# Attention forward in a transformer block: a fixed software pipeline with three score slots, value products two units behind, and the output turned by DMA

## The chip, the cores and the metric

The kernel runs on one core of a Trainium2 chip. The metric is the device time of one execution in microseconds (us). Before the change the median was 5007.97 us (three runs, 4999.35 to 5011.92).

Engines in the text: PE multiplies matrices, ACT evaluates exponentials, DVE and POOL do elementwise work, SP issues DMAs. PEld stands for PE's loading of weights. SBUF is the working memory; PSUM holds matmul results. A bank here is a piece of PSUM of 512 f32 columns, and the tile pools of both kernels come to eight of them.

## The reference

One block of a conditioned transformer, forward and backward: layer norm, attention with 32 heads of 16 channels over 2048 tokens, a squared-ReLU feed-forward, and the gradients of all of it. The change touches the attention forward alone:

```python
qkv = (x @ wqkv).reshape(B, S, 3, H, Dh)                    # S = 2048, H = 32, Dh = 16
scores = jnp.einsum('bhqd,bhkd->bhqk', q, k) * Dh ** (-0.5)
p = softmax(scores, axis=-1)
o = jnp.einsum('bhqk,bhkd->bhqd', p, v)
```

## The kernel before

Heads are handled four at a time (8 groups `hg`), queries in four blocks `qc` of 512, keys in sixteen tiles `kt` of 128. One such triple is a *unit*; there are 512. The *lag* is the number of units by which the value products run behind the scores. Per unit PE makes four score tiles (keys x queries). A head fills 32 of PE's 128 rows, so each score is a row-tiled matmul. ACT takes two score tiles per exponential (128x1024, two PSUM banks). PE then adds four value products, each 32 output columns wide (column-tiled), into one accumulator bank. `vaug` carries a column of ones, so the sum for the softmax comes along as a 17th row of each head.

```python
psS = tile_pool(name="psS", bufs=2, space=PSUM)     # two score slots of two banks
psO = tile_pool(name="psO", bufs=2, space=PSUM)     # two accumulators
psT = tile_pool(name="psT", bufs=1, space=PSUM)     # for the turn
for hg in range(HG):
    # ... load qt_sb, kt_sb of the group
    for qc in range(QC):
        oacc = psO.tile([P, 512], F32, tag="oacc")
        for kt in range(TT):
            ET = ework.tile([P, 4, 512], BF, tag="ET")
            for pair in range(2):
                ps = psS.tile([P, 2, 512], F32, tag="psST")
                for hi in range(2):
                    hq = 2 * pair + hi
                    PE.matmul(ps[:, hi, :], kt_sb[32*hq:32*hq+32, ...], qt_sb[32*hq:32*hq+32, ...],
                              tile_position=(32 * hq, 0))                         # L299
                ACT.activation(ET[:, 2*pair:2*pair+2, :], ps[:], AF.Exp, scale=SCALE)   # L302
            for hq in range(4):
                PE.matmul(oacc[32*hq:32*hq+32, :], lhsT, ET[:, hq, :],
                          start=(kt == 0), stop=(kt == TT - 1), tile_position=(0, 32 * hq))  # L306
        ostage = ...; DVE.tensor_copy(ostage[:], oacc[:])
        # ... rows of sums by DMA to rrows
        for qi in range(4):                              # turn the block: queries back to partitions
            pt = psT.tile([P, P], F32, tag="posT")
            PE.transpose(pt[:], ostage[:, qi*P:(qi+1)*P], identf[:])              # L317
            DVE.tensor_copy(O_un[...], pt...)                                     # L320
# ... for each token tile: transpose the sums, reciprocal, O_tok = O_un * r_inv
```

The order of instructions on each engine is not the program's order. A scheduler sets it: with two slots it issues the scores of one pair, then the value products of the pair before, and so on.

## Time and profile before

| stage | from to, us | length | bound by |
|---|---|---|---|
| preparation, projections | 0 to 292 | 292 | |
| attention forward | 292 to 1570 | 1278 | a loop between PE and ACT |
| feed-forward, its backward | 1570 to 2572 | 1002 | |
| attention backward | 2572 to 4720 | 2148 | |
| rest | 4720 to 5010 | 290 | |

The table of stretches of the kernel before. Columns: from:to, length, busy us (and instructions) of five engines, PEclk = granted PE clock as a share of full speed, DMA share, GB/s.

```profile
core 0: us, PE busy (x) PEld busy (x) DVE busy (x) ACT busy (x) POOL busy (x), PEclk, DMA share, GB/s
...
292.00:1570.00 1278.00, 1224.18 (x4236) 287.06 (x4237) 62.18 (x180) 1047.77 (x1025) 0.00 (x0) 0.50 0.02 6
...
2572.00:4720.00 2148.00, 1945.42 (x10240) 368.51 (x10239) 1222.26 (x1024) 1100.73 (x1185) 152.85 (x110) 0.61 0.73 136
```

In the forward ACT is busy 1048 of 1278 us and the matmul records cover 1224. The granted clock is 0.50 throughout. The page's groups, where the numbers after the bar are busy us and mean ns of one, then idle us before them and who ended it:

```profile
L302 ACT ACTIVATE ET<-psST 128x1024 bf16<-128x1024 f32 x1024 | 1046.5, 1024 | 228.4 <-PE psST L299 226.3
...
L299 PE MATMUL psST<-qt_sb,kt_sb 32*128 32x512 bf16 x2048 | 658.3, 603 | 17.3 <-DMA kt_sb<-KtP 17.3
L306 PE MATMUL oacc<-ET,vaug 128*32 128x512 bf16 x2048 | 626.1, 604 | 45.9 <-ACT ET L302 4.5
```

ACT idles 228 us, nearly all of it for scores. The timeline shows how (start, length, engine, line, what, count):

```profile
start us, us, engine line op out<-in xcount [idle before <-releaser]
800.10 1.02 ACT L302 ACTIVATE ET<-psST 128x1024 bf16<-128x1024 f32 x1
800.14 0.61 PE L306 MATMUL oacc<-ET,vaug 128*32 128x512 bf16 x2
...
800.69 0.61 PE L299 MATMUL psST<-qt_sb,kt_sb 32*128 32x512 bf16 x2
...
801.23 0.61 PE L306 MATMUL oacc<-ET,vaug 128*32 128x512 bf16 x2
801.39 2.04 ACT L302 ACTIVATE ET<-psST 128x1024 bf16<-128x1024 f32 x2 [0.28 <-PE psST L299]
...
801.77 0.61 PE L299 MATMUL psST<-qt_sb,kt_sb 32*128 32x512 bf16 x2
...
802.47 0.61 PE L306 MATMUL oacc<-ET,vaug 128*32 128x512 bf16 x2
...
803.72 1.02 ACT L302 ACTIVATE ET<-psST 128x1024 bf16<-128x1024 f32 x1 [0.28 <-PE psST L299]
```

The value products at 800.14 start just after an exponential that began at 799.07 ends (its record lasts 1.02). The scores at 800.69 follow. The exponential of those scores begins at 801.39, after an idle 0.28, and two of them run. The whole repeats after 2.33 us: 801.39 to 803.72. The chain is exponential ends, value pair, score pair, exponential: 0.06 + 0.55 + 0.70 + 1.02 = 2.33. PE alternates between the two tile forms four times a unit, at 0.54 us each.

The waits view (who waited for whom, us in total, times, longest):

```profile
ACT ET L302 <- PE psST L299: 226.3, 536, 1.8
...
PE psST L299 <- DMA kt_sb<-KtP: 17.3, 1, 17.3
```

The second line is the start of the stage: the first keys arrive late, behind two weight loads of 1.8 MB each.

### The profile page before, as it was taken

What the parts mean: (1) busy time and instruction counts of PE and PEld (TensorE: products, weight loads), DVE (VectorE), ACT (ScalarE), POOL (GpSimd) and SP (SyncE); (2) the same over time, 40 slices, a digit from 0 to 9 for tenths busy, and PEclk for the clock granted to TensorE, in tenths of its full rate; (3) what the DMA queues carried; (4) which work ended last, traced back from release to release, by engine and by line L of the source; (5) the groups of instructions that cost most, each with busy time, mean ns of one, the idle gap of its engine ahead of it and who ended that gap; (6) DMA issues with size and microseconds to landing.
All of it is one profiled execution on the core that took longest, in us unless ns stands there. A gap on an engine that the chain in (4) does not pass through costs nothing.

```text
span 5010.0 us, 48266 instructions
## 1 busy us (share of the span) xinstructions
PE 4158.7 (83%) x18556; PEld 1052.9 (21%) x18629; DVE 2069.8 (41%) x3264; ACT 2232.8 (45%) x2462; POOL 274.0 (5%) x282
## 2 busy tenths in 40 slices
PE   4789999999997872866579999998989999989766
PEld 1222222222222321322221111111111111111122
DVE  7610000000004752720336555555555555555473
ACT  0058888888884000000025555545554554555411
POOL 2000000000000000001310000010000000000000
PEclk7865555555555886966855565666565655666687
DMA  3220000000001243365467867777686877677513
GB/s 110 82 79 9 9 1 9 9 9 8 2 1 42 110 129 90 89 204 173 133 148 132 159 127 150 128 134 143 125 153 123 153 124 147 127 134 130 123 56 92
DMA packets 1212437, 489.34 MB, mean 98 GB/s; under 512 B 1144611, under 2 KB 1174823, under 8 KB 1210669
## 3 DMA queue, kind: packets, MB, share of 16 engines
q1 hardware_dynamic: 1189550, 455.84, 41.5%
q0 software_dynamic: 6144, 28.32, 1.9%
q10 hardware_dynamic: 16512, 2.10, 0.3%
q8 instruction: 146, 2.39, 0.2%
q14 instruction: 85, 0.70, 0.0%
HBM read 124.35 MB, written 80.37 MB: 41 GB/s over the span
## 4 chain that ended last, share of the span: by engine, by line
PE 33%; ACT 8%; DVE 5%; DMA 3%; issue 3%; SPq 1%; POOL 0%; ACTq 0%; DVEq 0%; POOLq 0%
PE psS_u L708 8%; PE accVK L736 8%; ACT E_u L710 7%; PE psD_u L714 6%; PE dqacc L762 5%; PE accVK L739 4%; DVE dS_u L716 3%; DMA dsT<-dS_u 1%; SPq L919 1%; DMA stld<-stok_st 0%; DVE dh1acc L831 0%; DVE dqkv_tok L823 0%; DMA out_dram<-w2blk 0%; ACT vktmp L747 0%; POOL dOs_tokpad L595 0%
## 5 line engine op out<-in xcount | busy, mean ns | idle before, releaser
L716 DVE TENSOR_TENSOR dS_u<-psD_u,E_u 128x1024 bf16<-128x1024 f32 x1024 | 1222.3, 1222 | 965.6 <-ACT E_u L710 780.2
L710 ACT ACTIVATE E_u<-psS_u 128x1024 bf16<-128x1024 f32 x1024 | 1018.6, 1023 | 886.3 <-PE psS_u L708 881.4
L302 ACT ACTIVATE ET<-psST 128x1024 bf16<-128x1024 f32 x1024 | 1046.5, 1024 | 228.4 <-PE psST L299 226.3
L714 PE MATMUL psD_u<-iv,ido 32*128 32x512 bf16 x2048 | 643.3, 540 | 107.7 <-ACT E_u L710 91.9
L299 PE MATMUL psST<-qt_sb,kt_sb 32*128 32x512 bf16 x2048 | 658.3, 603 | 17.3 <-DMA kt_sb<-KtP 17.3
L306 PE MATMUL oacc<-ET,vaug 128*32 128x512 bf16 x2048 | 626.1, 604 | 45.9 <-ACT ET L302 4.5
L708 PE MATMUL psS_u<-ik,iq 32*128 32x512 bf16 x2048 | 601.6, 532 | 22.5 <-ACT E_u L710 14.8
L309 DVE COPY ostage<-oacc 128x512 f32<-128x512 f32 x32 | 22.1, 692 | 1083.7 <-PE oacc L306 1083.7
L739 PE MATMUL accVK<-E_u,dOs_tok 128*16 128x512 bf16 x2048 | 462.9, 554 | 0.0
L762 PE MATMUL dqacc<-dsT,KS_tok 128*32 128x512 bf16 x2048 | 427.9, 605 | 12.5 <-DMA dsT<-dS_u 9.8
L736 PE MATMUL accVK<-dS_u,qz_14655 128*32 128x512 bf16 x1024 | 316.8, 543 | 35.5 <-DVE dS_u L716 35.3
L736 PE MATMUL accVK<-dS_u,qz_14654 128*32 128x512 bf16 x1024 | 303.7, 557 | 26.8 <-DVE dS_u L716 26.7
L708 PEld LDWEIGHTS <-iq 32*128 32x128 bf16 x2048 | 126.1, 96 | 663.8 <-issue 650.3
L306 PEld LDWEIGHTS <-vaug 128*32 128x32 bf16 x2048 | 151.7, 102 | 466.1 <-issue 437.5
L570 ACT ACTIVATE w1blk<-aw_0_13090 128x512 bf16<-128x512 f32 x1 | 0.6, 597 | 556.2 <-PE aw_0_13090 L566 556.2
L748 POOL TENSOR_TENSOR dVKacc<-dVKacc,vktmp 128x512 f32<-128x512 f32 x96 | 121.3, 1264 | 1910.0 <-ACT vktmp L747 1910.0
L714 PEld LDWEIGHTS <-ido 32*128 32x128 bf16 x2048 | 144.2, 100 | 331.6 <-issue 309.3
L299 PEld LDWEIGHTS <-kt_sb 32*128 32x128 bf16 x2048 | 111.4, 99 | 478.0 <-issue 478.0
L490 PE MATMUL pds<-gfT,w2T 128*128 128x512 bf16 x219 | 54.4, 400 | 109.6 <-DVE dzT L493 79.5
L736 PEld LDWEIGHTS <-qz_14655 128*32 128x32 bf16 x1024 | 59.1, 99 | 312.4 <-issue 311.9
L736 PEld LDWEIGHTS <-qz_14654 128*32 128x32 bf16 x1024 | 56.1, 99 | 295.8 <-issue 295.8
L262 PE MATMUL ppad<-xn1T,wpadT 128*128 128x512 bf16 x376 | 99.1, 409 | 21.7 <-DVE stagep L265 16.2
(1253 smaller groups left out, 2931.6 us busy)
## 6 DMA issues: line engine op xcount, KB each, us to landing
dzld<-dztok_st POOLq DMA_DIRECT2D x32, 448.0 KB, 3.7
dzld<-dztok_st SPq DMA_DIRECT2D x32, 448.0 KB, 3.6
dsT<-dS_u SPq DMA_TRANSPOSE x512, 4.3
rT_st<-rT SPq DMA_DIRECT2D x4, 1792.0 KB
rtok_st<-rtok SPq DMA_DIRECT2D x16, 448.0 KB, 2.5
stok_st<-stok SPq DMA_DIRECT2D x16, 448.0 KB
rTb<-rT_st SPq DMA_DIRECT2D x4, 1792.0 KB
rtokb<-rtok_st SPq DMA_DIRECT2D x16, 448.0 KB, 4.0
```

Of the source, the lines that this page charges most:

```text
L262: PE.matmul(pp[:], wpadT[:, ic, which, hg, :], h1T[:, ic, qc * 512:(qc + 1) * 512], start=(ic == 0), stop=(ic == DC - 1))
L299: PE.matmul(ps[:, hi, :], kt_sb[32 * hq:32 * hq + 32, kt * P:(kt + 1) * P], qt_sb[32 * hq:32 * hq + 32, qc * 512:(qc + 1) * 512], start=Tr ...
L302: ACT.activation(ET[:, 2 * pair:2 * pair + 2, :], ps[:], AF.Exp, scale=SCALE)
L306: PE.matmul(oacc[32 * hq:32 * hq + 32, :], lhsT, ET[:, hq, :], start=(kt == 0), stop=(kt == TT - 1), tile_position=(0, 32 * hq), skip_grou ...
L708: PE.matmul(psS[:, hi, :], st["q"][r:r + 32, qt * P:(qt + 1) * P], st["k"][r:r + 32, kc * 512:kc * 512 + 512], start=True, stop=True, tile ...
L710: ACT.activation(E_u[:, 2 * pair:2 * pair + 2, :], psS[:], AF.Exp, scale=SCALE)
L714: PE.matmul(psD[:, hi, :], st["do"][r:r + 32, qt * P:(qt + 1) * P], st["v"][r:r + 32, kc * 512:kc * 512 + 512], start=True, stop=True, til ...
L716: DVE.tensor_tensor(dS_u[:, 2 * pair:2 * pair + 2, :], psD[:], E_u[:, 2 * pair:2 * pair + 2, :], ALU.mult)
L736: PE.matmul(acc[32 * hq:32 * hq + 32, :], st["qz"][:, qt, hq, :], dS_u[:, hq, :], start=(qi == 0), stop=False, tile_position=(0, 32 * hq), ...
L739: PE.matmul(acc[32 * hq:32 * hq + DH, :], dOs_tok[:, qt, (hg * 4 + hq) * DH:(hg * 4 + hq + 1) * DH], E_u[:, hq, :], start=False, stop=(qi ...
L748: POOL.tensor_tensor(dst, dst, tmp[:], ALU.add)
L762: PE.matmul(acc[32 * hq:32 * hq + 32, :], KS_tok[:, kc * 4 + kt, h * DH:h * DH + 32], tT[:, hq * 4 + kt, :], start=(kc == 0 and kt == 0), ...
```

## The change

Its intent: cut the loop, so that ACT never waits. Three score slots take six banks. The two accumulators take the other two of the eight, so no bank is left for the turn (the transposition of a finished block, queries back to partitions). It goes to DMA, with a bf16 cast on POOL before it. The order on PE and ACT is fixed: both score pairs of unit u, then all four value products of unit u-2.

```diff
-        ework = ... tile_pool(name="phCe", bufs=3)
+        ework = ... tile_pool(name="phCe", bufs=4)
-        psS = ... tile_pool(name="psS", bufs=2, space=PSUM)
+        psS = ... tile_pool(name="psS", bufs=3, space=PSUM)
-        psT = ... tile_pool(name="psT", bufs=1, space=PSUM)
-        O_un = big.tile([P, TT, D], BF, name="O_un")
+        O_un = big.tile([P, TT, HG, P], BF, name="O_un")
+        def fscore(u):   # two pairs: row-tiled scores, exponential each (as before)
+        def fpv(u):      # four column-tiled value products (as before); at the block's end:
                 DVE.tensor_copy(ostage[:], oacc[:])
+                POOL.tensor_copy(obf[:], ostage[:])
-                for qi in range(4):
-                    PE.transpose(pt[:], ostage[:, qi * P:(qi + 1) * P], identf[:])
-                    DVE.tensor_copy(dst, src)
+                SP.dma_start(out=O_un[:, qc * 4:(qc + 1) * 4, hg, :], in_=obf[:], transpose=True)
+        with tc.manual_schedule(engines={PE.engine, ACT.engine}):
+            for u in range(NF + 2):
+                if u < NF:
+                    ...  # load the next head group in time
+                    fscore(u)
+                if u >= 2:
+                    fpv(u - 2)
```

Cut: the loads, and the final scaling, which reads the wider `O_un` and puts its transposes into the accumulators' banks.

More of the change, by code (lines that the diff above doesn't have):

```diff
@@ L277, with fload @@
         wk = ph.enter_context(tc.tile_pool(name="phC", bufs=2))
-        ework = ph.enter_context(tc.tile_pool(name="phCe", bufs=3))
+        ework = ph.enter_context(tc.tile_pool(name="phCe", bufs=4))
         big = ph.enter_context(tc.tile_pool(name="phCbig", bufs=1))
-        psS = ph.enter_context(tc.tile_pool(name="psS", bufs=2, space=bass.MemoryType.PSUM))
+        psS = ph.enter_context(tc.tile_pool(name="psS", bufs=3, space=bass.MemoryType.PSUM))
         psO = ph.enter_context(tc.tile_pool(name="psO", bufs=2, space=bass.MemoryType.PSUM))
-        psT = ph.enter_context(tc.tile_pool(name="psT", bufs=1, space=bass.MemoryType.PSUM))
         rrows = big.tile([P, n], F32, name="rrows")
-        O_un = big.tile([P, TT, D], BF, name="O_un")
-        for hg in range(HG):
+        O_un = big.tile([P, TT, HG, P], BF, name="O_un")
+        funits = [(hg, qc, kt) for hg in range(HG) for qc in range(QC) for kt in range(TT)]
+        fh, fe, fcur = {}, {}, {}
+        def fload(hg):
             qt_sb = wk.tile([P, n], BF, name="qt_sb", tag="qt_sb")
@@ L290 @@
             SP.dma_start(out=kt_sb[:], in_=KtP[hg])
-            for qc in range(QC):
-                oacc = psO.tile([P, 512], F32, name="oacc", tag="oacc")
-                for kt in range(TT):
-                    ET = ework.tile([P, 4, 512], BF, name="ET", tag="ET")
-                    for pair in range(2):
-                        ps = psS.tile([P, 2, 512], F32, name="psST", tag="psST")
-                        for hi in range(2):
-                            hq = 2 * pair + hi
-                            PE.matmul(ps[:, hi, :], kt_sb[32 * hq:32 * hq + 32, kt * P:(kt + 1) * P],
-                                      qt_sb[32 * hq:32 * hq + 32, qc * 512:(qc + 1) * 512],
-                                      start=True, stop=True, tile_position=(32 * hq, 0))
-                        ACT.activation(ET[:, 2 * pair:2 * pair + 2, :], ps[:], AF.Exp, scale=SCALE)
-                    for hq in range(4):
-                        h = hg * 4 + hq
-                        lhsT = vaug[:, kt].rearrange("p h c -> p (h c)")[:, h * (DH + 1):h * (DH + 1) + 32]
-                        PE.matmul(oacc[32 * hq:32 * hq + 32, :], lhsT, ET[:, hq, :],
-                                  start=(kt == 0), stop=(kt == TT - 1), tile_position=(0, 32 * hq), skip_group_check=True)
@@ new lines, in fload @@
+            fh[hg] = (qt_sb, kt_sb)
+        def fscore(u):
+            hg, qc, kt = funits[u]
+            qt_sb, kt_sb = fh[hg]
+            ET = ework.tile([P, 4, 512], BF, name="ET", tag="ET")
+            fe[u] = ET
+            pss = []
+            for pair in range(2):
+                ps = psS.tile([P, 2, 512], F32, name="psST", tag="psST")
+                for hi in range(2):
+                    r = 32 * (2 * pair + hi)
+                    PE.matmul(ps[:, hi, :], kt_sb[r:r + 32, kt * P:(kt + 1) * P],
+                              qt_sb[r:r + 32, qc * 512:(qc + 1) * 512],
+                              start=True, stop=True, tile_position=(r, 0))
+                ACT.activation(ET[:, 2 * pair:2 * pair + 2, :], ps[:], AF.Exp, scale=SCALE)
@@ new lines, in fpv @@
+        def fpv(u):
+            hg, qc, kt = funits[u]
+            if kt == 0:
+                fcur["o"] = psO.tile([P, 512], F32, name="oacc", tag="oacc")
+            oacc = fcur["o"]
+            ET = fe.pop(u)
+            for hq in range(4):
+                h = hg * 4 + hq
+                lhsT = vaug[:, kt].rearrange("p h c -> p (h c)")[:, h * (DH + 1):h * (DH + 1) + 32]
+                PE.matmul(oacc[32 * hq:32 * hq + 32, :], lhsT, ET[:, hq, :],
+                          start=(kt == 0), stop=(kt == TT - 1), tile_position=(0, 32 * hq), skip_group_check=True)
+            if kt == TT - 1:
@@ L308 @@
                 ostage = wk.tile([P, 512], F32, name="ostage", tag="ostage")
                 DVE.tensor_copy(ostage[:], oacc[:])
+                obf = wk.tile([P, 512], BF, name="obf", tag="obf")
+                POOL.tensor_copy(obf[:], ostage[:])
                 for hq in range(4):
@@ L313 @@
                                  in_=ostage[32 * hq + 16:32 * hq + 17, :])
-                for qi in range(4):
-                    t = qc * 4 + qi
-                    pt = psT.tile([P, P], F32, name="posT", tag="posT")
-                    PE.transpose(pt[:], ostage[:, qi * P:(qi + 1) * P], identf[:])
-                    src = pt.rearrange("q (h c) -> q h c", h=4)[:, :, 0:DH]
-                    dst = O_un[:, t, hg * 64:(hg + 1) * 64].rearrange("q (h d) -> q h d", h=4)
-                    DVE.tensor_copy(dst, src)
-        for t in range(TT):
-            pr = psT.tile([P, H], F32, name="prinv", tag="prinv")
-            PE.transpose(pr[:], rrows[0:H, t * P:(t + 1) * P], identf[0:H, 0:H])
-            DVE.reciprocal(r_inv[:, t, :], pr[:])
-            DVE.tensor_tensor(O_tok[:, t, :].rearrange("p (h d) -> p h d", d=DH),
-                              O_un[:, t, :].rearrange("p (h d) -> p h d", d=DH),
-                              r_inv[:, t, :].unsqueeze(2).to_broadcast([P, H, DH]), ALU.mult)
+                SP.dma_start(out=O_un[:, qc * 4:(qc + 1) * 4, hg, :], in_=obf[:], transpose=True)
+        NF = len(funits)
+        fload(0)
+        with tc.manual_schedule(engines={PE.engine, ACT.engine}):
+            for u in range(NF + 2):
+                if u < NF:
+                    if funits[u][1:] == (2, 0) and funits[u][0] + 1 < HG:
+                        fload(funits[u][0] + 1)
+                    fscore(u)
+                if u >= 2:
+                    fpv(u - 2)
+        for t in range(TT):
+            pr = psO.tile([P, 512], F32, name="prinv", tag="oacc")
+            PE.transpose(pr[:, 0:H], rrows[0:H, t * P:(t + 1) * P], identf[0:H, 0:H])
+            DVE.reciprocal(r_inv[:, t, :], pr[:, 0:H])
+            DVE.tensor_tensor(O_tok[:, t, :].rearrange("p (g h d) -> p g h d", g=HG, h=4),
+                              O_un[:, t].rearrange("p g (h c) -> p g h c", h=4)[:, :, :, 0:DH],
+                              r_inv[:, t, :].rearrange("p (g h) -> p g h", g=HG).unsqueeze(3).to_broadcast([P, HG, 4, DH]),
+                              ALU.mult)
         SP.dma_start(out=o_st[:], in_=O_tok[:])
```

## The prediction

It was written before the changed kernel ran.

> What bounds the kernel now. The table of stretches puts the attention forward at 292 to 1570 us, 1278 of 5010 us. There ACT is busy 1048 us, matmuls 1224 us at a granted clock of 0.50. Neither engine is at its limit: the timeline repeats every 2.33 us per unit (four heads, one key tile; 512 units). In it ACT runs two exponentials of 1.02 us and idles 0.28 us for the scores (the waits give 226 us in all), and value products start as an exponential ends. With two score slots this is a loop: exponential ends, value pair (0.55 us), score pair, exponential 0.70 us after that score begins and lasting 1.02: 0.06+0.55+0.70+1.02 = 2.33. PE changes between row-tiled scores and column-tiled value products four times a unit, 0.54 us each: 2.16 us.
>
> What the change does.
> 1. Six banks hold three score slots; a unit's two score pairs stand together, then four value products of two units earlier, whose exponentials are long done. The loop is cut. PE per unit, from groups in the backward, which already has this form: score pair after score pair 0.43, a pair or quad with change of form 0.54: 0.43+0.54+0.54, about 1.5 us, up to 1.7 with weight-load stalls of 0.16.
> 2. ACT then bounds. Its exponential lasts 1.024 us, but in the backward's pairs the second starts 0.904 us after the first (two take 1.94). The Trainium skill, "Perfetto Trace Analysis", section "Optimizing Scalar/DVE Operations", says that half of the profiled access latency overlaps with the next instruction; the trace agrees (1.024 against 0.904). The forward's 1.02 spacing is the score's arrival (0.64 us after its start), not ACT's limit. So a unit should take 1.81 to 1.84 us: 1024 exponentials in about 932 us, against 1275 now. Gain about 340 us.
> 3. A score can start when the exponential three back ends and is needed 0.64 us before its own; three slots leave about 1 us of slack, more than the value quad takes. ACT should not starve.
> 4. PE loses 128 f32 transposes (0.47 us each), DVE 128 copies (0.22); mostly hidden now. Added: 32 casts on POOL (estimate below 1 us, from 0.65 for a bf16 copy) and 32 DMA transposes (4.3 us to landing in the backward), hidden but for the last. The tail from the last value product to O_tok, now 9 us, becomes about 11.
> 5. SBUF placement moves the two feed-forward weight loads (1.8 MB each) from before the first score load to after the stage. Now PE waits 17.3 us for kt_sb behind them; I expect 5 us back. Afterwards they run under the output projection.
> The rest keeps its instructions (ACT and POOL identical, PE and DVE reordered only in the projection): 5008 less 340, less 5, plus some 3.
>
> Predicted: 4666 us, 80% range 4640 to 4765. Faster by over 2%: 0.97; within 2%: 0.025; slower: 0.005.
>
> What would show it. Forward stage about 935 us; ACT busy about 99% of it, exponentials starting every 0.904 to 0.92 us; ACT idle for scores under 10 us; PE matmul busy share down to 75 to 90%, PE waiting for ACT; value products in quads of one modelled length, not two; clock still near 0.5. Backward (2570 to 4740) unchanged in length within 5 us.
>
> What would make it wrong. If every second exponential, which carries an extra wait for ACT's own earlier write, does not overlap with its predecessor, a unit takes 1.93 and the total is about 4730. If no overlap is sustained, 1.02 each: about 4780. If value quads do not run side by side, PE takes 1.95 a unit. The twelve early reciprocal transposes in the last query block could stall PE; late weight loads could delay the layer norm by up to 10 us.

## The result, and the profile after

| | before | after |
|---|---|---|
| median, us | 5009.94 (4 runs) | 4657.15 (4 runs, 4652.79 to 4670.40) |
| ratio | 1 | 0.930 (95% interval 0.9273 to 0.9328) |
| first score to last value product | 1277.6 | 941.4 |
| first to last exponential's start | 1273.9 | 937.1 |
| unit, median | 2.327 | 1.833 |

A ratio is formed from the fast runs of both kernels in the same rounds, so it isn't quite the ratio of the medians quoted. Lengths of stages are taken from the start and end times in the trace.

The stretches after, with the columns of before (forward; attention backward):

```profile
281.40:1223.00 941.60, 869.47 (x4111) 163.68 (x4112) 33.27 (x56) 940.05 (x1025) 19.06 (x31) 0.50 0.05 13
...
2230.00:4370.00 2140.00, 1941.20 (x10162) 366.19 (x10161) 1211.13 (x1015) 1089.05 (x1173) 152.72 (x110) 0.60 0.73 135
```

The profiled execution became 353 us shorter: 336 us in the forward stage and 11 us from its earlier start (281.5 instead of 292.1). The other 7 us lie in stages with unchanged work. From the last value product to the first exponential of the backward it was 988 us in place of 1006, and the exponentials of the backward spanned 2149 in place of 2135. Over all profiled kernels these two lengths scatter from 988 to 1006 and from 2132 to 2158, so nothing is read from that part.

The groups of the page:

```profile
L309 ACT ACTIVATE ET<-psST 128x1024 bf16<-128x1024 f32 x1024 | 938.8, 1770 | 0.0
...
L306 PE MATMUL psST<-qt_sb,kt_sb 32*128 32x512 bf16 x2048 | 622.5, 597 | 79.9 <-DMA kt_sb<-KtP 8.9
...
L320 PE MATMUL oacc<-ET,vaug 128*32 128x512 bf16 x2048 | 316.8, 609 | 0.6 <-ACT ET L309 0.6
```

Two traps stand here. The mean length of an exponential's record is now 1770 ns, though all but nine of the exponentials start 904 to 921 ns after the one before (median 911): the records overlap here, and the spacing, or busy time over count (938.8/1024 = 0.917 us), is what counts. The ends of the records are steadier than their starts: 916 to 918 ns apart. And the score matmuls' records still cover 622 us. The timeline:

```profile
799.64 5.49 ACT L309 ACTIVATE ET<-psST 128x1024 bf16<-128x1024 f32 x5
800.21 0.62 PE L320 MATMUL oacc<-ET,vaug 128*32 128x512 bf16 x4
...
800.77 1.35 PE L306 MATMUL psST<-qt_sb,kt_sb 32*128 32x512 bf16 x4
...
802.05 0.62 PE L320 MATMUL oacc<-ET,vaug 128*32 128x512 bf16 x4
...
802.60 1.35 PE L306 MATMUL psST<-qt_sb,kt_sb 32*128 32x512 bf16 x4
```

ACT runs without a gap. PE gives a value quad, then two score pairs whose records fill 1.35 us because the second pair waits for its slot: in the trace it starts 0.05 us after the end of the exponential three back. The waits in the stage show hardly any of that, and no wait of ACT for scores:

```profile
PE psST L306 <- ACT ET L309: 2.6, 3, 2.0
```

The start, one line of the timeline: PE waits 8.90 us for the first keys instead of 17.31.

```profile
281.46 1.04 PE L306 MATMUL psST<-qt_sb,kt_sb 32*128 32x512 bf16 x6 [8.90 <-DMA kt_sb<-KtP]
```

### The profile page after: what moved, and what is told of

Its sections match the earlier page's. It is cut to its first block, busy times and chain, and to the rows that moved or that the text cites. A ratio compares the mean times of both kernels' runs of the same rounds, so it can differ in the third digit from the quotient of the medians.

```text
span 4656.5 us, 48021 instructions
## 1 busy us (share of the span) xinstructions
PE 3802.4 (82%) x18427; PEld 924.4 (20%) x18501; DVE 2039.2 (44%) x3136; ACT 2125.7 (46%) x2462; POOL 293.9 (6%) x314
## 4 chain that ended last, share of the span: by engine, by line
PE 36%; ACT 8%; DVE 5%; DMA 4%; issue 3%; SPq 1%; POOL 0%; ACTq 0%; DVEq 0%; POOLq 0%
PE psS_u L731 9%; PE accVK L759 9%; ACT E_u L733 7%; PE psD_u L737 6%; PE dqacc L785 6%; PE accVK L762 4%; DVE dS_u L739 3%; DMA dsT<-dS_u 1%; SPq L942 1%; DVE dqkv_tok L846 1%; DMA stld<-stok_st 1%; DVE dh1acc L854 0%; DMA out_dram<-w2blk 0%; ACT vktmp L770 0%; POOL dOs_tokpad L618 0%
## 5 line engine op out<-in xcount | busy, mean ns | idle before, releaser
L309 ACT ACTIVATE ET<-psST 128x1024 bf16<-128x1024 f32 x1024 | 938.8, 1770 | 0.0
L306 PE MATMUL psST<-qt_sb,kt_sb 32*128 32x512 bf16 x2048 | 622.5, 597 | 79.9 <-DMA kt_sb<-KtP 8.9
L320 PE MATMUL oacc<-ET,vaug 128*32 128x512 bf16 x2048 | 316.8, 609 | 0.6 <-ACT ET L309 0.6
L785 PEld LDWEIGHTS <-KS_tok 128*32 128x32 bf16 x2048 | 79.2, 113 | 176.4 <-issue 165.9
```

The costliest lines, as they stand in the source:

```text
L306: PE.matmul(ps[:, hi, :], kt_sb[r:r + 32, kt * P:(kt + 1) * P], qt_sb[r:r + 32, qc * 512:(qc + 1) * 512], start=True, stop=True, tile_posi ...
L309: ACT.activation(ET[:, 2 * pair:2 * pair + 2, :], ps[:], AF.Exp, scale=SCALE)
L320: PE.matmul(oacc[32 * hq:32 * hq + 32, :], lhsT, ET[:, hq, :], start=(kt == 0), stop=(kt == TT - 1), tile_position=(0, 32 * hq), skip_grou ...
L785: PE.matmul(acc[32 * hq:32 * hq + 32, :], KS_tok[:, kc * 4 + kt, h * DH:h * DH + 32], tT[:, hq * 4 + kt, :], start=(kc == 0 and kt == 0), ...
```

## The experiments

The experiments ran in four groups, each on one chip with the kernel before beside it: two slots, both lags and the pairs; the DMA turn alone, with the third slot, the PE turn and the 384 columns; the order left to the scheduler, the changed kernel again and the triples; the 128 columns. Ratios are to that kernel. The runs that the table leaves out stand in their sections below.

| kernel | median, us | ratio | forward stage in the trace, us | unit, us |
|---|---|---|---|---|
| before | 5010 | 1 | 1277.6 | 2.327 |
| changed | 4657 | 0.930 | 941.4 | 1.833 |
| two slots | 4692 | 0.936 | 973.6 | 1.893 |
| lag of one unit | 4668 | 0.931 | 942.0 | 1.833 |
| no lag | 5384 | 1.075 | 1662.0 | 3.240 |
| value products in pairs | 4836 | 0.965 | 1108.2 | 2.160 |
| before + DMA turn | 4916 | 0.981 | 1194.6 | 2.327 |
| before + DMA turn + third slot | 4824 | 0.963 | 1108.4 | 2.160 |
| changed, order left to the scheduler | 4826 | 0.962 | 1108.5 | 2.160 |
| changed, PE turn | 4746 | 0.947 | 1009.3 | 1.808 |

The theory: the loop is cut by having value products far enough behind, PE's four changes of form are halved by grouping, and then ACT's exponentials bound the stage. Rivals: the third slot feeds ACT (A); slots and DMA turn make the gain and the order doesn't (B); grouping is indifferent (C).

### Two score slots

```diff
-psS = tile_pool(name="psS", bufs=3)
+psS = tile_pool(name="psS", bufs=2)
```

> The changed kernel with two score slots in PSUM instead of three, all else as it is. My theory: the lag and the grouping matter, the third slot hardly. Stepping the groups by hand with the measured durations (score 0.64 us before its exponential can start, slot free 1.07 us after its exponential starts, 0.43 us from score pair to score pair, 0.54 us at a change of form), a unit takes 1.85 us instead of 1.81: about 20 us more, 4660 to 4720, with ACT idle 10 to 60 us for scores. Rival A, that the third slot is what keeps ACT fed: most of the gain goes, 4850 or more.

Measured 4691.79 us, ratio 0.936 (0.9338 to 0.9381); the stage is 32 us longer. Rival A falls: with lag and grouping in place the third slot is worth about a tenth of the stage's gain. PE now shows the wait for its slot; the second score pair often starts late:

```profile
701.38 0.62 PE L320 MATMUL oacc<-ET,vaug 128*32 128x512 bf16 x4
...
702.08 0.61 PE L306 MATMUL psST<-qt_sb,kt_sb 32*128 32x512 bf16 x2
702.99 0.61 PE L306 MATMUL psST<-qt_sb,kt_sb 32*128 32x512 bf16 x2 [0.30 <-ACT ET L309]
```

The expectation of ACT's idle time was missed: ACT shows 2 us, not 10 to 60. The loss sits in the spacing (968.8 us busy in place of 938.8), as an exponential whose score is late doesn't overlap with the one before.

### A lag of one unit, and none

```diff
-            for u in range(NF + 2):  ...  if u >= 2: fpv(u - 2)
+            for u in range(NF + 1):  ...  if u >= 1: fpv(u - 1)     # and with 0
```

> The changed kernel with the value products one unit behind the scores instead of two. My theory: the value quad's exponentials end about 0.95 us after its last score starts, PE waits there for half a microsecond that it has to spare, and with three slots ACT still finds a score ready: no change, within 8 us of the changed kernel (4650 to 4668). Rival, that two units of lag are needed: 20 us or more slower.

Measured 4668.38 us, ratio 0.9313 (0.9292 to 0.9334), against 0.930 for the changed kernel; the median is 0.4 us outside of what was expected (4650 to 4668). The stage decides: 942.0 against 941.4 us. One unit of lag is enough, and the second one isn't used.

> The changed kernel with the value products right after their own unit's scores (no lag); three slots, fixed order and DMA turn stay. My theory: the lag is what cuts the loop. PE then waits for both exponentials of the unit and ACT then waits for the next scores: 0.64 + 0.91 + 1.07 + 0.54 = 3.15 us a unit, about 690 us more, 5330 (5250 to 5400), slower than the kernel before. Rival B, that slots and DMA turn make the gain: stays under 4800.

Measured 5384.49 us, ratio 1.0748: slower than the kernel before, with three slots, DMA turn and grouping all in place. Rival B falls. The loop stands in the timeline: PE waits 1.17 us for the exponential before its value products, ACT 1.30 us for the scores after them.

```profile
699.38 1.94 ACT L309 ACTIVATE ET<-psST 128x1024 bf16<-128x1024 f32 x2 [1.30 <-PE psST L306]
...
700.45 0.61 PE L320 MATMUL oacc<-ET,vaug 128*32 128x512 bf16 x2 [1.17 <-ACT ET L309]
...
701.37 0.61 PE L320 MATMUL oacc<-ET,vaug 128*32 128x512 bf16 x2 [0.30 <-ACT ET L309]
...
701.91 0.61 PE L306 MATMUL psST<-qt_sb,kt_sb 32*128 32x512 bf16 x4
...
702.62 1.94 ACT L309 ACTIVATE ET<-psST 128x1024 bf16<-128x1024 f32 x2 [1.30 <-PE psST L306]
```

### Value products in pairs

```diff
-                fscore(u)                 # two pairs
-                fpv(u - 2)                # four products
+                fscore(u, 0); fpv(u - 2, 0)   # a pair each
+                fscore(u, 1); fpv(u - 2, 1)
```

> The changed kernel with the same lag and slots, but the value products in two pairs, one after each score pair, so that PE changes form four times a unit as in the kernel before. My theory: each group costs PE 0.54 us, 2.16 us a unit, and PE bounds instead of ACT: 512 x (2.16 - 1.83), about 170 us more, 4825 (4790 to 4850); ACT idle about 170 us for scores. Rival C, that grouping is indifferent once the loop is cut: 4650 to 4670.

Measured 4836.12 us, ratio 0.965 (0.9631 to 0.9669). The unit is 2.160 us, as four changes of 0.54. Each line below starts 0.54 us after the one above:

```profile
699.83 0.60 PE L306 MATMUL psST<-qt_sb,kt_sb 32*128 32x512 bf16 x2
...
700.37 0.61 PE L320 MATMUL oacc<-ET,vaug 128*32 128x512 bf16 x2
...
700.91 0.61 PE L306 MATMUL psST<-qt_sb,kt_sb 32*128 32x512 bf16 x2
...
701.45 0.61 PE L320 MATMUL oacc<-ET,vaug 128*32 128x512 bf16 x2
...
701.99 0.61 PE L306 MATMUL psST<-qt_sb,kt_sb 32*128 32x512 bf16 x2
```

Rival C falls: a pair and a quad cost PE the same 0.54 us, so half of the groups is half of the time. The Trainium skill, "TensorEngine Tiling (Array Packing)", section "Key Properties", says "Mode switching requires drain"; the trace agrees: at this clock, groups of two and of four, each with a change of form, follow each other by 0.54 us, while quads of one form (`dqacc` in the backward of the kernel before, same clock) follow each other by 0.39 to 0.43 us. ACT's idle time again came out smaller than expected (61 us, not 170), for the reason above.

### The kernel before with the DMA turn alone

```diff
-                for qi in range(4):  PE.transpose(...); DVE.tensor_copy(...)
+                POOL.tensor_copy(obf[:], ostage[:])
+                SP.dma_start(out=O_un[...], in_=obf[:], transpose=True)
```

> The kernel before with only the output's turn moved from PE to DMA; two slots, the scheduler's order of pairs, no fixed order. The prediction called the 128 PE transposes mostly hidden. In the trace of before, the exponentials around each query block's end are spaced up to 2.86 us instead of 1.3: 102 such gaps sum to 76 us beyond the rhythm. If they come from the transposes in PE's order, this kernel gains about 76 us, and some 8 from the weight loads that move away from the start: about 4925 (4905 to 4950). If the transposes were hidden: 5000 or more.

Measured 4915.99 us, ratio 0.9809 (0.979 to 0.9828): clearly below 1, though about the 2% that a verdict asks for. The stage is 83 us shorter while the unit keeps its 2.327 us: all of it comes from the ends of query blocks. ACT's idle time fell by as much, from 228.4 us:

```profile
L302 ACT ACTIVATE ET<-psST 128x1024 bf16<-128x1024 f32 x1024 | 1046.5, 1024 | 145.5 <-PE psST L299 143.3
```

The stage also starts 10 us earlier, since the weight loads moved here too. In the kernel before, such an end reads:

```profile
810.70 2.04 ACT L302 ACTIVATE ET<-psST 128x1024 bf16<-128x1024 f32 x2 [0.28 <-PE psST L299]
...
811.93 0.47 PE L317 MATMUL posT<-identf,ostage 128*128 128x128 f32 x1 [0.25 <-DVE ostage L309]
...
813.41 0.47 PE L317 MATMUL posT<-identf,ostage 128*128 128x128 f32 x1
...
814.52 1.02 ACT L302 ACTIVATE ET<-psST 128x1024 bf16<-128x1024 f32 x1 [1.77 <-PE psST L299]
...
815.43 0.47 PE L317 MATMUL posT<-identf,ostage 128*128 128x128 f32 x1
...
816.37 0.47 PE L317 MATMUL posT<-identf,ostage 128*128 128x128 f32 x1
816.47 1.02 ACT L302 ACTIVATE ET<-psST 128x1024 bf16<-128x1024 f32 x1 [0.93 <-PE psST L299]
...
818.02 2.04 ACT L302 ACTIVATE ET<-psST 128x1024 bf16<-128x1024 f32 x2 [0.53 <-PE psST L299]
```

The exponentials start at 810.70 (two, the second about 1.02 later), 814.52, 816.47 and 818.02: up to 2.8 us apart instead of at most 1.31, while f32 transposes stand between scores on PE. So the transposes were not hidden, as the prediction had said.

### The DMA turn and the third slot, order left to the scheduler; and the changed kernel without its fixed order

```diff
 before + DMA turn, and: psS bufs=2 -> 3, no psT, prinv in psO, ework bufs=3 -> 4
 changed kernel:  with tc.manual_schedule(...):  ->  if True:
```

> The kernel before with the DMA turn and a third score slot, order left to the scheduler, which then runs value pairs three score pairs behind instead of two, but still as alternating pairs. My theory: the loop is cut by the third slot here, and PE bounds with four changes of form a unit, 2.16 us: about as the split one, 4825 (4790 to 4860). Rival A (slots make the gain): about 4660. If the fixed order is what cuts the loop: about 4925, as with the DMA turn alone.

> The changed kernel without the fixed order on PE and ACT; the scheduler then runs alternating pairs, value pairs four score pairs behind. Theory: slots and lag are there, grouping is not, so PE bounds with four changes of form, 2.16 us a unit as the split one: 4830 (4800 to 4850). If the fixed order adds nothing: 4657.

Measured 4824.32 us (ratio 0.9632) and 4825.88 us (0.9619), stages 1108.4 and 1108.5 us. Left to itself, the scheduler alternates pairs in both. When a value pair is issued, six score matmuls (in the first kernel) or eight (in the second) have been issued since its own first score, that one included; in the kernel before it was four. The loop is cut by the third slot's longer lag, and PE's four changes bound at 2.160. The fourth buffer of `ET` came in the same edit; the trace shows at most two in use at once in the first kernel, as before, so it isn't the cause. The fixed order is what makes quads of the pairs: it is worth 167 us.

So the 336 us of the stage add up, in this order of steps: 83 for the DMA turn (1277.6 to 1194.6), 86 for the third slot with the lag that it allows (to 1108.4), 167 for the grouping (to 941.4). In another order the shares would differ: with the grouping in place, the third slot is worth only 32.

### The changed kernel with the PE turn

```diff
-psO bufs=2
+psO bufs=1; psT bufs=1          # six banks are in the score slots
-POOL cast, DMA transpose
+four PE.transpose and DVE copies, in PE's order before the next block's second value quad
```

> The changed kernel with the output turned by PE again (four f32 transposes and four DVE copies per query block, in PE's order before the second value quad of the next block; one accumulator bank and one transpose bank instead of two accumulators). Theory: four transposes with one bank take PE about 3.2 us in a row (0.79 us each at the end of the kernel before), and PE also waits some 0.9 us for the single accumulator; ACT's stock of scores and PE's spare time cover about half: 50 to 90 us more, 4700 to 4750. If the transposes hide, under 4670.

Measured 4745.7 us, ratio 0.9469 (0.9448 to 0.9489), stage 68 us longer: 2.1 us of idle ACT at each of 31 block ends (64.6 us in all). The bank and the turn can't be told apart by this run: it has one accumulator, and the transposes have one bank. The lines after the last transpose held a surprise:

```profile
699.14 0.48 PE L335 MATMUL posT<-identf,ostage 128*128 128x128 f32 x1 [0.38 <-DVE O_un L336]
...
699.54 0.62 PE L321 MATMUL oacc<-ET,vaug 128*32 128x512 bf16 x4
...
700.10 0.61 PE L307 MATMUL psST<-qt_sb,kt_sb 32*128 32x512 bf16 x4
...
700.64 0.62 PE L321 MATMUL oacc<-ET,vaug 128*32 128x512 bf16 x4
700.80 1.02 ACT L310 ACTIVATE ET<-psST 128x1024 bf16<-128x1024 f32 x1 [2.08 <-PE psST L307]
```

Catching up, PE does four scores in 0.54 us and four value products in 0.56 us, 1.1 us a unit. The prediction had put 1.5, counting score pairs one after another. The run without lag shows the same in every unit: its four scores start within 0.01 us of each other (`x4` at 701.91 above).

### Shorter exponentials

Both are wrong: fewer columns of each score tile are exponentiated, and the value products read other columns of the tile, so PE's work stays.

```diff
+FW = 384                                        # then 128
-ACT.activation(ET[:, 2*pair:2*pair+2, :], ps[:], AF.Exp, scale=SCALE)
+ACT.activation(ET[... 2*FW columns], ps[:, :, 0:FW], AF.Exp, scale=SCALE)
```

> Wrong on purpose: the changed kernel with exponentials of 384 of each 512 columns; the value products read other columns of the same tile, so PE's work is unchanged. My theory: ACT bounds the changed kernel. The exponential's spacing falls from 0.91 to about 0.70 us (256 elements at 0.83 ns less), 1.40 us a unit, and PE bounds next at 0.43+0.54+0.54 = 1.51: about 155 us less than the changed kernel, 4500 (4470 to 4540). If PE bounded the changed kernel already, the time would hardly move (4640 or more).

Measured 4445.97 us, ratio 0.8869. The time followed ACT's work, so ACT did bound the changed kernel. But PE did not stop it at 1.51: the unit is 1.407 us, which is ACT's spacing again (median 0.706), and ACT never idled; the kernel came out faster than expected (4470 to 4540).

```profile
L310 ACT ACTIVATE ET<-psST 128x768 bf16<-128x768 f32 x1024 | 720.7, 957 | 0.1
```

The expectation's 0.83 ns an element comes out of the trace before: an ACTIVATE of 1024 columns takes 1024 ns there, one of 512 columns 597 ns, which is 0.834 ns a column.

> Wrong on purpose: the changed kernel with exponentials of 128 of each 512 columns, PE's work unchanged, to measure what a unit costs PE when ACT is out of the way. The prediction said 0.43+0.54+0.54 = 1.51 us a unit; then the forward stage takes about 775 us. In the burst with which the PE-turn kernel caught up, four scores and then four value products took 0.54 us each, four side by side: then a unit takes 1.08 to 1.15 us and the stage 555 to 590 us, the whole 4275 to 4310.

Measured 4132.65 us (two runs), unit 0.848 us: below both expectations. The reason stands in the stretch (columns as in the table of stretches before), in the seventh place after the length:

```profile
285.00:680.00 395.00, 394.60 (x3980) 130.15 (x3978) 21.44 (x31) 327.37 (x997) 18.44 (x30) 0.99 0.11 28
```

The granted clock is 0.99 in the stage. In every other variant it was 0.50. With full clock the quads follow each other faster than 0.54 us. So the 1.1 us a unit at half clock, seen in the burst above, was not confirmed here; only that PE can do a unit in less than 1.51 is shown. What raised the clock is open: more matmuls in the same time are the obvious guess, and no run isolates it. The share of time with a matmul record is not it: with value products in pairs that was 1105 of 1107 us at 0.50.

### Exponentials over three heads

If ACT bounds, its fixed cost per instruction is what is left to take. Two slots of three banks, exponentials of 128x1536:

```diff
-psS bufs=3, tiles [P, 2, 512]; ET [P, 4, 512] x 4
+psS bufs=2, tiles [P, 3, 512]; ET [P, 12, 512] x 3     # three units = four triples
```

> The changed kernel once more, to stand beside the next one on the same chip: 4645 to 4670.

> The changed kernel with exponentials over three heads (128x1536, three banks) and two score slots of three banks, value quads once their triples are two behind. If ACT's element rate and a fixed cost per instruction bound the stage, spacing becomes 1536 x 0.833 + 51 = 1.33 us, 683 of them: about 910 us in place of 938, some 28 us less, 4630 (4615 to 4645), 0.5 to 0.7% faster than the changed kernel. If two slots leave ACT waiting (exponential's start to slot free 1.5, value quad up to 0.54, score 0.64: 2.68 against 2.66 for two exponentials), it gains nothing or loses: 4655 to 4700.

The changed kernel took 4665.5 us (five runs, ratio 0.9297), the triples 4653.35 us (four runs, 4649.88 to 4655.98, ratio 0.9275, 0.9257 to 0.9293), both correct. The medians differ by 12 us, a quarter of a per cent, and the intervals of the ratios overlap, though each of the four runs is faster than each of the five. The time missed the expectation of 4615 to 4645: 12 us were gained, not 28. In the trace the stage shrank by 22, 919.8 against 941.4 us. The expectation's fixed cost was too small: 51 ns is what 904 ns, the shortest spacing of two starts, leaves beyond 1024 times 0.833. The ends of the exponentials are 1.343 us apart, against 0.917 before; with 1.343 the 683 exponentials take 917 us, not 910.

```profile
L314 ACT ACTIVATE ET<-psST 128x1536 bf16<-128x1536 f32 (+1 forms) x683 | 917.2, 1907 | 0.0
```

```profile
PE psST L309 <- ACT ET L314: 214.6, 663, 2.4
```

PE now waits for its slots 215 us, without harm. By its median it is the fastest correct kernel, by little.

## Why the prediction was right or wrong

The time was right: 4666 predicted, 4657 measured, and the forward stage, "about 935 us", was 941.4.

- **The loop and its cut: right.** No lag brings a loop back (3.240 us a unit), one unit of lag suffices, and ACT's wait for scores, 226 us before, is gone.
- **ACT bounds, spacing 0.904 to 0.92: right.** The trace has 904 to 921 ns, 916 on average. The case where every second one doesn't overlap did not come. The Trainium skill's sentence on overlap ("Perfetto Trace Analysis", "Optimizing Scalar/DVE Operations") agrees with the trace in that there is one, 1.024 alone against 0.917 in a row; its "half" is not shown: of the 170 ns that a 1024-column record takes beyond 0.834 ns a column, 107 overlap.
- **"Gain about 340 us": right in size, 337 from first to last exponential, but put down to the wrong causes.** The prediction gave all of it to the loop, by taking the stage's whole length before. A unit's shortening gives 512 x (2.327 - 1.833) = 253 us. The step that failed is "mostly hidden now" for the PE transposes: the run with the DMA turn alone shows them to have cost 83 us at the ends of query blocks. The sum came out all the same, because the prediction subtracted the stage's whole length after from its whole length before, and the transposes were in the latter.
- **PE at "about 1.5 us, up to 1.7" a unit: mis-sized.** Its term of 0.43 for a score pair behind a score pair is too large: four scores run side by side like four value products. The burst shows 1.1. The 0.43 came from the backward, where the two row-tiled pairs that stand in a row (`psS_u`, then `psD_u`) read the same rows of PE (`32 * (2 * pair + hi)` in both) and start 0.39 to 0.40 us apart; a unit's pairs in the forward read different rows and start 0.01 us apart when nothing holds them. That the rows make the difference is read from the code, and no run tests it alone. It did no harm, as ACT bounds either way.
- **"Three slots leave about 1 us of slack": right but not needed.** A pair starts 2.52 to 2.70 us before its exponential ends, 0.9 to 1.0 more than the 0.64 and 1.02 that it needs. Two slots cost 32 us of the stage.
- **"PE busy share down to 75 to 90%, PE waiting for ACT": wrong as a reading.** The records cover 869 of 942 us, 92%, and 3 us of waiting are shown, though PE had room. The Trainium skill ("Perfetto Trace Analysis", section "Identifying the Most-Contended Engine") calls matmul busy time a bad measure of how close a kernel is to its roofline; the runs agree: the changed kernel and the triples are both bound by ACT, with records over 92% and 76% of the stage.
- **Start and tail.** 5 us expected from the weight loads, 10.6 measured, of which 8.4 in the wait for keys. Cast 0.615 us (below 1, right); the DMA transpose landed in 2.4 us, not the backward's 4.3; from the last value product to the finished output it took 8.8 us, as before, and not 11.
- **Backward unchanged within 5 us: not shown.** It was 14 us longer in this trace, inside the scatter over kernels that don't change it.

## What to carry to other kernels

When two engines take turns, write the chain of one round with lengths from the timeline. If it adds up to the period, no engine is at its limit, and letting the consumer lag one round behind is what pays; more buffers help mostly as far as they allow that lag (86 us where the third slot brought it, 32 where it was there already). On PE, put matmuls of one tile form together: two and four side by side cost the same here. And judge the new limit by the spacing of the limiting instructions, not by the length of their records or by a busy share; shortening their work, even wrongly, shows in one run which engine bounds.

## What the Trainium skill lacked or had wrong

- "ScalarE: Activation LUTs" ("What ACT_TABLE_LOAD costs") gives an ACTIVATE with immediate scale and bias 186 ns + 0.833 ns an element and an overlap of about 93 ns back to back. It doesn't say for which memories. Reading PSUM and writing SBUF, 1024 columns took 1024 ns alone, 15 ns less, and 917 ns back to back, an overlap of 107 ns. With 703 ns for 768 columns and 1343 ns for 1536 (all from the ends of the records) the spacing fits 0.832 ns an element and about 65 ns.
- "TensorE: Matmul & The Clock Gate" (Part 1) says that activity releases the clock, not what counts as activity for row- and column-tiled matmuls. Here the clock stayed at 0.50 for 1278 us with matmul records over 96% of them (and for 1107 us with records over all of them, value products in pairs). It was 0.99 when the same number of such matmuls came in 408 us, with ACT's work cut to a quarter of the columns.
- "TensorEngine Tiling (Array Packing)" gives no cost for its drain at a change of form: at the half clock, groups of two or four 512-column matmuls with a change each were spaced 0.54 us, and quads without a change 0.39 to 0.43 us.
- "Perfetto Trace Analysis" says that the write-acknowledgement half of an access latency overlaps with the next instruction. It doesn't say that ACT's records can overlap by far more: they lasted 1816 ns at the median for exponentials started every 0.911 us.
